# Seven products for eight in both MLP layers, over two token passes of 1024, with the second pass's token forms kept in DRAM

## The chip, the core and the metric

One NeuronCore of a Trainium2 chip runs the whole program. Its engines have instruction queues of their own, each worked off in order: TensorE (PE for the matmuls, PEld for its weight loads), VectorE (DVE), ScalarE (ACT), GpSimd (POOL) and SyncE (SP, which here issues every DMA). The metric is the device time of one execution in microseconds.

## The reference

A block with two residual branches on 2048 tokens of 576 features, float32: a spectral filter, then a two-layer MLP with a ReLU between (4608 hidden columns).

```python
def _A_ref(x, w_r, w_i):
    B, S, D = x.shape                       # 1, 2048, 576
    X = jnp.fft.rfft2(x, axes=(-2, -1)) * (w_r + 1j * w_i)
    return jnp.fft.irfft2(X, (S, D), axes=(-2, -1))

def _B_ref(x, w1, w2):                      # w1 576 x 4608, w2 4608 x 576
    h = jnp.maximum(jnp.einsum("bsd,df->bsf", x, w1), 0)
    return jnp.einsum("bsf,fd->bsd", h, w2)

h = x + _A_ref(_layernorm(x), w_r, w_i)
h2 = h + _B_ref(_layernorm(h), w1, w2)
```

## The kernel before

The transforms are matmuls with constant tables and take the first 115 us. From there a loop over 16 tiles of 128 tokens (`for t in range(NT + 6)`) ends the inverse transform (`inv_d`, `inv_a`), adds the residual into the tile `A` (`xs`), takes the layer norm (`stat2`, `norm2`) and transposes the result into `xc` (`project`).

A float32 product is made of three matmuls in float32r: an operand v is split into a high part h (a copy to float32r, on ACT) and a low part v - h (a subtraction, on DVE); a product is hh + hl + lh. `split` (L305 to L307; the copy itself is L151, in `act`) does that for weights and hidden blocks.

The MLP goes over 18 groups of 256 hidden columns (`g`) and four chunks of 512 tokens (`c`): 72 steps. `mm1` makes a step's hidden block: per 128 hidden columns 14 matmuls of 512 columns (L148, operands `xc` and the split weights). For the first eight steps `mm2` multiplies with w2 directly. From step 8 on (`WINO = 8`) `slot` does the second layer with seven products of half blocks in place of eight (Winograd's form of Strassen's algorithm): sums of the halves of the hidden block (S1 to S4) and of w2 (T1 to T4), each split; `prod` (L562) makes a product in 6 matmuls of 288 columns, and `add` (L569) adds it from PSUM into one or two quarters of `xs`. Such a slot alternates four quarters of the next step's `mm1` (7 matmuls each) with the seven products. The hidden sums are made on POOL (L547, L551 to L553), the weight sums also (L519). The order on every engine is the order in which the code is written (`manual_schedule`).

Tiles that matter: `A` the residual and result, `X` the split weight forms, `D` the split hidden forms, `e` a rotating buffer of ten, `d` four PSUM tiles of two banks.

Of the kernel before, what the change touches and what calls it, by code (L numbers as in the profile page):

```python
# [21 lines left out]
GF = 2  # L22
NG = DFF // (128 * GF)
CH = 4
NC = NT // CH
# [102 lines left out]
def kernel(ctx: ExitStack, tc: tile.TileContext, x, w_r, w_i, w1, w2, cc2, c1, fb, ib, c3, out):  # L128
    nc = tc.nc
    pool = ctx.enter_context(tc.tile_pool(name="sb", bufs=1))  # L130
    psum = ctx.enter_context(tc.tile_pool(name="ps", bufs=1, space=PSUM))

    def sb(shape, tag, bufs=1, dt=F32):
        n[0] += 1
        return pool.tile(shape, dt, tag=tag, name=f"{tag}_{n[0]}", bufs=bufs)

    n = [0]

    def ps():
# [13 lines left out]
    xs = sb([128, NT, D], "X")  # L153
# [70 lines left out]
    zx = sb([128, 5 * 2048], "A")  # L224
# [69 lines left out]
    raw, wts = {}, {}  # L294

    def load_weights(g):
        v1, v2 = ebuf([128, 5, 256]), ebuf([128, 2, D])
        f = slice(256 * g, 256 * g + 256)
        nc.sync.dma_start(v1[:, 0:4], w1[0:512, f].rearrange("(a p) f -> p a f", p=128))
        for h in range(2):  # L300
            nc.sync.dma_start(v1[64 * h:64 * h + 64, 4], w1[512:576, f])
        nc.sync.dma_start(v2, w2[f, :].rearrange("(a p) d -> p a d", p=128))
        raw[g] = (v1, v2)

    def split(h, l, v):  # L305
        act(h, v)
        nc.vector.tensor_sub(l, v, h)  # L307

    pieces = []

    def work(k):
        for _ in range(k):
            split(*pieces.pop(0))

    def split_weights(g, part):
        if g == 1 and part == 0:
            h, l = tail[0][:, 4608:5888], tail[0][:, 5888:7168]
        else:
            h, l = (ebuf([128, (1280, 1152)[part]], F32R) for _ in range(2))
        h, l = (v.rearrange("p (a n) -> p a n", a=(5, 2)[part]) for v in (h, l))  # L320
        wts[g, part] = h, l
# [304 lines left out]
    def slot(i):  # L626
# [12 lines left out]
        if w1:  # L639
            work(1)  # L640
# [130 lines left out]
```

## Time and profile before

| | |
|---|---|
| device time, median of 3 runs | 1054.95 us (1054.93 to 1055.49) |
| span of the profiled execution | 1053.3 us, of a time that is not listed apart; the median is 1.65 us above it |
| granted TensorE clock, mean | 0.994 |
| busy: PE, PEld, DVE, ACT, POOL | 1036.2, 928.0, 750.3, 389.9, 328.0 us |
| slots of the second layer in seven products | from 290 to 1047 us, 11.91 us each |
| DMA | 48.05 MB, mean 46 GB/s |

Busy times count an engine's instructions only. Matmuls overlap each other, so the duration of one (294 ns for 288 columns) is longer than the distance to the next. A group's row has line, engine, operation, written and read tiles, sizes, count, busy time and the mean of one, and then the idle time ahead of it with what ended it. A timeline row has start, duration, and the same. For back-to-back instructions the distance of two starts is the price.

### The profile page before, as it was taken

The page shows a single profiled execution, that of the slowest core. Times are in us where ns is not written, and L with a number is a line of the kernel's source. Part 1 is how long each engine was busy: PE and PEld are TensorE (multiplying, and loading weights), DVE is VectorE, ACT ScalarE, POOL GpSimd, SP SyncE. Part 2 cuts the span into 40 slices and gives each one's busy share as a digit, 9 for nine tenths or more (in the row PEclk, how much of TensorE's full clock was granted, in tenths as well). Part 3 has the DMA queues.
Part 4 walks back from the last instruction along what each step waited for, and adds up shares of the span by engine and source line. Part 5 has one row for each costly group of instructions (what it writes and reads, how often), then busy time and mean ns, then how long its engine had stood idle before and what let it go on. Part 6 is the DMA issues. An engine that isn't in the chain of part 4 may idle for free.

```text
span 1053.3 us, 17197 instructions
## 1 busy us (share of the span) xinstructions
PE 1036.2 (98%) x6560; PEld 928.0 (88%) x6560; DVE 750.3 (71%) x1409; ACT 389.9 (37%) x846; POOL 328.0 (31%) x439
## 2 busy tenths in 40 slices
PE   8999999999999999999999999999999999999997
PEld 8888778799999999999999999999999999999996
DVE  7587696543477777778777777778777777777775
ACT  4533243431133333334333333434333333434332
POOL 4300164311133424333333423333333323243322
PEclk9999999999999999999999999999999999999999
DMA  8931700011000011000000001000000001100024
GB/s 239 248 92 49 180 2 26 23 48 48 1 26 23 26 36 36 26 23 26 24 26 23 26 24 48 26 23 26 24 26 23 26 24 40 34 23 2 1 63 117
DMA packets 31105, 48.05 MB, mean 46 GB/s; under 512 B 2992, under 2 KB 22704, under 8 KB 31024
## 3 DMA queue, kind: packets, MB, share of 16 engines
q1 hardware_dynamic: 31024, 46.96, 16.5%
q8 instruction: 52, 0.85, 0.3%
q14 instruction: 29, 0.24, 0.1%
HBM read 42.23 MB, written 4.72 MB: 45 GB/s over the span
## 4 chain that ended last, share of the span: by engine, by line
PE 95%; DVE 3%; ACT 1%; issue 0%; POOL 0%; DVEq 0%; POOLq 0%; ACTq 0%
PE d L148 60%; PE d L562 33%; PE d L276 1%; PE d L446 1%; DVE A L569 0%; DVE A L428 0%; DVE e L307 0%; DVE e L416 0%; DVE e L415 0%; ACT e L222 0%; DVE e L419 0%; DVE e L360 0%; DVE e L359 0%; PE d L447 0%; DVE e L354 0%
## 5 line engine op out<-in xcount | busy, mean ns | idle before, releaser
L569 DVE TENSOR_TENSOR A<-A,d 128x576 f32<-128x576 f32 (+1 forms) x449 | 334.5, 746 | 52.6 <-PE d L562 52.5
L562 PE MATMUL d<-X,D 128*128 128x288 f32 x2304 | 345.8, 294 | 1.8 <-DVE A L569 1.7
L562 PEld LDWEIGHTS d<-X,D 128*128 128x128 f32 x2304 | 328.8, 188 | 17.3 <-issue 1.7
L148 PE MATMUL d<-B,e 128*128 128x512 f32 x952 | 238.3, 391 | 0.4 <-DVE A L428 0.4
L148 PEld LDWEIGHTS d<-B,e 128*128 128x128 f32 x952 | 172.0, 188 | 28.8 <-ACT e L151 0.8
L537 DVE SCALAR_TENSOR_TENSOR D<-d,D 128x256 fp32r<-128x256 f32 x190 | 80.7, 425 | 120.6 <-ACT D L536 120.6
L536 ACT ACTIVATE D<-d 128x256 fp32r<-128x256 f32 x190 | 72.6, 382 | 237.6 <-PE d L148 237.6
L551 POOL TENSOR_TENSOR e<-e 128x256 f32<-128x256 f32 x63 | 46.6, 739 | 349.8 <-ACT e L550 349.8
L148 PE MATMUL d<-C,e 128*128 128x512 f32 x476 | 119.1, 390 | 0.0
L148 PE MATMUL d<-X,e 128*128 128x512 f32 x476 | 118.7, 390 | 0.0
L151 ACT ACTIVATE X<-e 128x288 fp32r<-128x288 f32 (+2 forms) x177 | 70.2, 434 | 103.5 <-PE d L562 103.5
L307 DVE TENSOR_TENSOR D<-e,D 128x256 fp32r<-128x256 f32 (+1 forms) x128 | 92.6, 724 | 20.1 <-ACT D L151 20.1
L547 POOL TENSOR_TENSOR e<-e 128x256 f32<-128x256 f32 x64 | 47.5, 743 | 173.8 <-ACT e L546 170.5
L148 PEld LDWEIGHTS d<-X,e 128*128 128x128 f32 x476 | 86.0, 188 | 13.8
L148 PEld LDWEIGHTS d<-C,e 128*128 128x128 f32 x476 | 85.8, 188 | 13.7
L151 ACT ACTIVATE D<-e 128x256 fp32r<-128x256 f32 (+1 forms) x130 | 67.4, 519 | 75.3 <-POOL e L552 70.4
L307 DVE TENSOR_TENSOR X<-e,X 128x288 fp32r<-128x288 f32 (+2 forms) x176 | 82.8, 493 | 0.9 <-ACT X L151 0.9
L562 PEld LDWEIGHTS d<-X 128*128 128x128 f32 x384 | 58.0, 188 | 4.9
L562 PE MATMUL d<-X 128*128 128x288 f32 x384 | 61.3, 295 | 0.0
L148 PE MATMUL d<-e,D 128*128 128x288 f32 x384 | 55.3, 303 | 0.3 <-DVE D L480 0.3
L148 PEld LDWEIGHTS d<-e,D 128*128 128x128 f32 x384 | 53.7, 194 | 1.4 <-DVE D L480 0.6
L552 POOL TENSOR_TENSOR e<-e,e 128x256 f32<-128x256 f32 x63 | 49.7, 788 | 4.9
(85 smaller groups left out, 994.4 us busy)
## 6 DMA issues: line engine op xcount, KB each, us to landing
e<-in_B_w_dram SPq DMA_DIRECT2D x18, 576.0 KB, 3.8
e<-in_B_w_dram SPq DMA_DIRECT2D x18, 512.0 KB, 3.7
A<-in_A_x_dram SPq DMA_DIRECT2D x16, 288.0 KB, 8.2
out_dram<-A SPq DMA_DIRECT2D x30, 144.0 KB, 2.5
X<-in_A_x_dram SPq DMA_DIRECT2D x12, 288.0 KB, 7.4
e<-in_B_w_dram SPq DMA_DIRECT2D x36, 64.0 KB, 3.5
B<-in_A_w_r_dram SPq DMA_DIRECT2D x15, 144.5 KB, 7.3
B<-in_A_w_i_dram SPq DMA_DIRECT2D x15, 144.5 KB, 7.2
```

Source lines behind the costliest of these rows:

```text
L148: nc.tensor.matmul(o, l, r, start=start, stop=stop)
L151: nc.scalar.activation(o, i, AF.Copy, **kw)
L276: nc.tensor.transpose(wm[:, :128], ident, ident)
L307: nc.vector.tensor_sub(l, v, h)
L446: nc.tensor.transpose(pz[:, 128 * b:128 * b + 128], y[:, 128 * b:128 * b + 128], ident)
L536: nc.scalar.activation(h, p, AF.Relu)
L537: nc.vector.scalar_tensor_tensor(l, p, 0.0, h, op0=ALU.max, op1=ALU.subtract)
L547: nc.gpsimd.tensor_sub(fs["S3"], fs["p0"][:, 0], fs["p0"][:, 1])
L551: nc.gpsimd.tensor_add(fs["S1"], fs["p0"][:, 1], fs["p1"][:, 1])
L552: nc.gpsimd.tensor_sub(fs["S2"], fs["S1"], fs["p0"][:, 0])
L562: nc.tensor.matmul(P[:, tt], l[:, q], r, start=first and n_ == 0, stop=n_ == 2, skip_group_check=not first)
L569: nc.vector.tensor_add(xt, xt, P)
```

## The change

Both layers now use seven half-block products for eight. The tokens are taken in two passes of 1024, the hidden columns in steps of 512: 18 steps (`NS`), nine per pass, of 14 slots each. A slot is one of the first layer's seven products (`mm1`, for one of two halves u of 256 hidden columns), what combines its result (`evac`), the split of the hidden form that is needed two slots later (`form`), one product of the second layer for the step before (`prod`), and at fixed slots hidden sums and splits of weights (`tasks_old`, `tasks_new`).

- First layer: the 512 leading features and the tokens are halved; `norm2` makes four sums of the normed tokens on POOL, `project` transposes eight blocks twice per pair of tiles and splits them into seven forms `T`; the remaining 64 features stay apart in `R`. `sums1` (POOL) and `split1` make the weight forms `WF`. A product is 6 matmuls of 512 columns, plus 2 for the rest in four of the seven. Results come out of two PSUM banks, `X` and `Y`: ACT copies three partial sums (s1, u2, u3), DVE adds `Y` to them (L556), ACT applies the relu in place (L557), or reads `X` with it (L552).
- Second layer: hidden sums move from POOL to DVE (`hsum`, L520) and the products are over 512 hidden columns: 12 matmuls of 288 columns (L569) accumulate both halves `j`; the adds into `xs` are L574. Weight sums of 576 elements (`sums2`, L501) stay on POOL.
- The second pass's seven forms are written to DRAM (`Td`, 28 stores of 256 KB) while step 0 runs, and read back in step 8 (7 loads of 1 MB).
- The first layer starts at iteration 16 of the loop over tiles (iteration 10 before), since a pass needs the forms of eight tiles. PSUM: three rotating tiles `d`, and the banks `X` and `Y`, in place of four.

```diff
-GF = 2
-NG = DFF // (128 * GF)
-CH = 4
-NC = NT // CH
+NS = 18
...
+        nc.gpsimd.tensor_sub(S[:, 0], b12, b11)
+        nc.gpsimd.tensor_sub(S[:, 2], b22, b12)
+        nc.gpsimd.tensor_sub(S[:, 1], b22, S[:, 0])
+        nc.gpsimd.tensor_sub(S[:, 3], b21, S[:, 1])
+        Zs[t0 // 2] = z, S
...
+        for a, b, dst in dsts:
+            act(dst[:, :, 0], pv[:, a:b])
+            nc.vector.tensor_sub(dst[:, :, 1], pv[:, a:b], dst[:, :, 0])
...
+        if P:
+            for a, b, dst in dsts:
+                for f in range(a, b):
+                    nc.sync.dma_start(Td[f0 + f, :, :, i % 4], dst[:, f - a].rearrange("p h k n -> p (h k) n").bitcast(F32))
...
+    ORDER = (("A11", 0), ("A12", 1), ("S2", 4), ("S1", 3), ("S3", 5), ("A22", 6), ("S4", 2))
+    BANK = (0, 1, 0, 1, 0, 0, 1)
...
+    PRODS = [(n_[:2], "ab".index(n_[2])) for n_ in "P1a P2a P1b P2b P6a P5a P6b P3a P7a P5b P7b P3b P4a P4b".split()]
...
+    def form(s, k):
+        p, x = PRODS[k]
+        q = SIDE[p][0]
+        f = HF[(14 * s + k) % 4]
+        split(f[:, 0], f[:, 1], raw(s, INPLACE.get(q, q))[:, :, 256 * x:256 * x + 256])
+
+    def mm1(s, u, m):
+        a, b = ORDER[m]
+        o = M["XY"][BANK[m]]
+        ops = []
+        for k in range(2):
+            w = [WF[:, i, BLOCK[a] + k] for i in range(2)]
+            t = [T[:, b, i, k] for i in range(2)]
+            ops += [(w[0], t[0]), (w[0], t[1]), (w[1], t[0])]
...
+        for n_, (l, r) in enumerate(ops):
+            nc.tensor.matmul(o, l, r, start=first and n_ == 0, stop=n_ == len(ops) - 1, skip_group_check=not first)
+
+    def evac(s, u, m):
...
+        if m in (0, 2, 4):
+            act((s1, u2, u3)[m // 2], X)
+        if m == 5:
+            nc.scalar.activation(raw(s, q0, 1), X, AF.Relu)
+        if m in (1, 4, 6):
+            a, q, j = {1: (s1, q0, 0), 4: (u3, q1, 1), 6: (u2, q1, 0)}[m]
+            h = raw(s, q, j)
+            nc.vector.tensor_add(h, a, Y)
+            nc.scalar.activation(h, h, AF.Relu)
+
+    def prod(s, k):
...
+        for tt in range(2):
+            ops = [(l, r, j) for j in range(2) for l, r in ((0, 0), (0, 1), (1, 0))]
+            for n_, (l, r, j) in enumerate(ops):
+                nc.tensor.matmul(o[:, tt], f[:, l, j, 128 * tt:128 * tt + 128], w[:, r, j], start=first and n_ == 0,
+                                 stop=n_ == 5, skip_group_check=not first)
+        t0 = 8 * (s // 9) + c + 4 * x
+        tiles, d = slice(t0, t0 + 3, 2), slice(288 * hd, 288 * hd + 288)
+        xt = xs[:, tiles, d]
+        nc.vector.tensor_add(xt, xt, o)
...
+    def tasks_old(s, k):
+        if k == 0:
+            hsum(s, "S1", 0)
+            hsum(s, "S2", 1)
+        if k == 1:
+            hsum(s, "S2", 0)
+        if k in (2, 3):
+            split2(s, ("T2", "T1")[k - 2])
+            hsum(s, "S4", k - 2)
+        if k == 5:
+            split2(s, "B22")
+            split2(s, "T3")
+        if k == 8:
+            split2(s, "T4")
+
+    def tasks_new(s, k):
+        u, m = divmod(k, 7)
+        v = 2 * s + u
+        if v and k == 7:
+            split1(v, 1)
+        if v and k in (1, 7):
+            split1(v, 3)
+        if m == 0 and v + 2 < 2 * NS:
+            load1(v + 2)
+        if v + 1 < 2 * NS:
+            if m in (1, 2):
+                sums1(v + 1, m - 1)
+            if k in (4, 6, 10, 12, 13):
+                split1(v + 1, {4: 0, 6: 2, 10: 0, 12: 2, 13: 1}[k])
...
+        if k == 9:
+            hsum(s, "S3")
+        if k == 11:
+            split2(s, "B11")
+            sums2("T1", "T3", "T2")
+        if k == 12:
+            hsum(s, "S1", 1)
+        if k == 13:
+            split2(s, "B21")
+            sums2("T4")
+        if s == 8 and u == 1:
+            b = ORDER[m][1]
+            nc.sync.dma_start(T[:, b].rearrange("p h k n -> p (h k n)").bitcast(F32), Td[b].rearrange("p a i n -> p (a i n)"))
+
+    def slot(S, k):
+        if S < NS:
+            mm1(S, *divmod(k, 7))
+            evac(S, *divmod(k, 7))
+            if k >= 12:
+                form(S, k - 12)
+        if S:
+            if k < 12:
+                form(S - 1, k + 2)
+            prod(S - 1, k)
+            tasks_old(S - 1, k)
+        if S < NS:
+            tasks_new(S, k)
```

`split1` takes 640, 384, 512 and 640 elements for its four parts, `split2` 576, `form` 512.

What that makes of DVE's queue in the middle of the run. Before, a slot's rows: splits of hidden blocks from PSUM (L537), product adds (L569), and splits of hidden sums and weights from SBUF (L307):

```order
L537 SCALAR_TENSOR_TENSOR D_2581<-d_2580,D_2581 128x256
L569 TENSOR_TENSOR A_1268<-A_1268,d_2688 128x2x288
L537 SCALAR_TENSOR_TENSOR D_2582<-d_2580,D_2582 128x256
L569 TENSOR_TENSOR A_1268<-A_1268,d_2688 128x2x288
L307 TENSOR_TENSOR D_2583<-e_2585,D_2583 128x512
L569 TENSOR_TENSOR A_1268<-A_1268,d_2689 128x2x288
L537 SCALAR_TENSOR_TENSOR D_2581<-d_2579,D_2581 128x256
L569 TENSOR_TENSOR A_1268<-A_1268,d_2688 128x2x288
L307 TENSOR_TENSOR D_2582<-e_2585,D_2582 128x256
L569 TENSOR_TENSOR A_1268<-A_1268,d_2689 128x2x288
L307 TENSOR_TENSOR X_1872<-e_5078,X_1872 128x288 x2
L569 TENSOR_TENSOR A_1268<-A_1268,d_2688 128x2x288
```

After, the slots 11 and 12 of a step and the add that opens slot 13: the first layer's add (L556), the hidden form's split into `G` (L467), the product add (L574), the split of B11, then the next slot's form, add and tasks:

```order
L556 TENSOR_TENSOR h_4515<-u_298_1844,Y 128x512
L467 TENSOR_TENSOR G_2215<-h_4119,G_2215 128x512
L574 TENSOR_TENSOR A_1284<-A_1284,d_2218 128x2x288
L467 TENSOR_TENSOR e_2213<-e_1958,e_2213 128x576
L467 TENSOR_TENSOR HF_1851<-h_4234,HF_1851 128x512
L574 TENSOR_TENSOR A_1284<-A_1284,d_2216 128x2x288
L467 TENSOR_TENSOR WF_1288<-e_1507,WF_1288 128x512
L520 TENSOR_TENSOR h_4318<-h_4318,h_4515 128x512
L556 TENSOR_TENSOR h_4515<-u_297_1843,Y 128x512
```

Between a first-layer add and the product add behind it there is now a split that reads an ACT result. ACT's queue at the same place, before (a hidden block's relus L536, its whole relu for POOL L546 and L550, splits L151):

```order
L536 ACTIVATE D_2581<-d_2580 128x256
L550 ACTIVATE e_2584<-d_2580 128x512
L536 ACTIVATE D_2582<-d_2580 128x256
L151 ACTIVATE D_2583<-e_2585 128x512
L536 ACTIVATE D_2581<-d_2579 128x256
L546 ACTIVATE e_2584<-d_2579 128x512
L151 ACTIVATE D_2582<-e_2585 128x256
```

and after (from the partial sum u3 of slot 11 to the copy for slot 13's form):

```order
L161 ACTIVATE u_298_1844<-X 128x512
L557 ACTIVATE h_4515<-h_4515 128x512
L161 ACTIVATE G_2215<-h_4119 128x512
L161 ACTIVATE e_2213<-e_1958 128x576
L552 ACTIVATE h_4433<-X 128x512
L161 ACTIVATE HF_1851<-h_4234 128x512
L161 ACTIVATE WF_1288<-e_1507 128x512
L557 ACTIVATE h_4515<-h_4515 128x512
L161 ACTIVATE e_2117<-h_4433 128x512
```

The relu in place (L557) stands ahead of the copy of the form (L161 into `G`, `HF`, `e_2117`) of the same slot. POOL's queue in one step, before (hidden sums of a chunk, and weight sums L519):

```order
L547 TENSOR_TENSOR e_2585<-e_2584 128x256
L551 TENSOR_TENSOR e_2585<-e_2584 128x256
L552 TENSOR_TENSOR e_2585<-e_2585,e_2584 128x256
L553 TENSOR_TENSOR e_2585<-e_2584,e_2585 128x256
L519 TENSOR_TENSOR e_3229<-e_2993 128x288 x2
```

and after (weight sums of the first layer for one half, then of the second layer):

```order
L480 TENSOR_TENSOR e_1507<-e_1506 128x256
L481 TENSOR_TENSOR e_1507<-e_1507,e_1506 128x256
L483 TENSOR_TENSOR e_1507<-e_1506 128x256
L484 TENSOR_TENSOR e_1507<-e_1506,e_1507 128x256
L485 TENSOR_TENSOR e_1507<-e_1506 128x128
L501 TENSOR_TENSOR e_1958<-e_1958 128x576
L501 TENSOR_TENSOR e_1958<-e_1961,e_1958 128x576
L501 TENSOR_TENSOR T_300_1852<-e_1961,e_1958 128x576
L501 TENSOR_TENSOR e_1961<-e_1961,T_300_1852 128x576
```

The hidden sums are gone from POOL's queue, and weight sums of 576 elements stand in a row behind those of the first layer.

More of the change, by code (lines that the diff above doesn't have):

```diff
@@ L293 @@
     nc.sync.dma_start(c3t, c3)
[L294 to L321, printed above, removed]
-        for k in range((5, 2)[part]) if g >= 2 else [slice(None)]:
-            pieces.append((h[:, k], l[:, k], raw[g][part][:, k]))
-        if g <= 2:
-            work(len(pieces))
-    tail = []
-    U = sb([128, 160 * 64], "X")
+    U = sb([128, 160 * 64], "X", pool="x")
     Xs, Ys = {}, {}
@@ L692 @@
         if t % 2 == 1 and 5 <= t <= NT + 3:
[L693 removed]
+            gen = norm2(t - 5)
             next(gen)
```

473 lines of the change are left out of this document (182 added, 291 removed).

## The prediction, made before the changed kernel ran

> **What bounds the kernel now.** I read the page's busy shares and its chain of waits first.
>
> ```profile
> span 1053.3 us, 17197 instructions
> PE 1036.2 (98%) x6560; PEld 928.0 (88%) x6560; DVE 750.3 (71%) x1409; ACT 389.9 (37%) x846; POOL 328.0 (31%) x439
> ...
> PE 95%; DVE 3%; ACT 1%; issue 0%; POOL 0%; DVEq 0%; POOLq 0%; ACTq 0%
> ```
>
> TensorE (PE) is busy 98% of the span and is 95% of the chain that ended last, so PE's work is what the change can remove; the other engines matter only if one of them takes PE's place. Then the windows over four consecutive slots of the second half (start and end, then PE, PEld, DVE, ACT and POOL busy time):
>
> ```profile
> 610.34:622.25 11.91, 11.91 (x71) 10.81 (x71) 9.21 (x18) 4.93 (x12) 2.96 (x4) 1.00 0.00 1
> 622.25:634.16 11.91, 11.91 (x71) 10.81 (x71) 9.39 (x17) 4.59 (x11) 3.17 (x4) 1.00 0.18 55
> 634.16:646.07 11.91, 11.91 (x71) 10.81 (x71) 8.91 (x17) 4.51 (x11) 5.02 (x6) 1.00 0.01 2
> 646.07:657.98 11.91, 11.91 (x72) 10.80 (x71) 8.57 (x16) 4.21 (x10) 5.07 (x6) 1.00 0.18 51
> sum 47.64, PE 47.64 PEld 43.23 DVE 36.08 ACT 18.24 POOL 16.22; mean PE 11.91 PEld 10.81 DVE 9.02 ACT 4.56 POOL 4.06
> ```
>
> Four slots are 512 hidden columns for 1024 tokens, as much as one step of the changed kernel: 47.64 us, PE without a hole, DVE busy for 36.08 of them, POOL 16.22. Prices on PE, from the timeline inside a slot:
>
> ```profile
> 603.03 1.75 PE L562 MATMUL d<-X,D 128*128 128x288 f32 x12
> 604.61 1.75 PE L148 MATMUL d<-X,e 128*128 128x512 f32 x7
> 606.20 0.96 PE L562 MATMUL d<-X 128*128 128x288 f32 x6
> ```
>
> 12 products of 288 columns take 604.61 - 603.03 = 1.58 us, 0.1317 each; 7 of 512 columns take 1.59, 0.227 each. Check: 4 x (28 x 0.227 + 42 x 0.1317) = 47.5, the measured 47.64.
>
> **What the change does to PE.** The first layer goes from 14 matmuls of 512 columns per 128 hidden columns and 512 tokens (56 per 256 x 1024) to 7 x 6 + 4 x 2 = 50: 1800 in all for 2016. The second layer was already seven products for eight in all but the first eight slots: 3024 of 288 columns for 3072. A step (14 slots) costs 100 x 0.227 + 168 x 0.1317 = 44.83 us on PE, 2.8 less than four slots now. If PE stays the bound, that is the gain, 6%.
>
> **What it does to DVE, ACT and POOL.** This is where I expect the sum to be decided. Every product now reads its own split of a hidden block, the first layer needs its outputs combined, and the weights of both layers are combined and split. Durations, start to start, from timeline rows:
>
> ```profile
> 126.39 1.48 DVE L307 TENSOR_TENSOR e<-e,e 128x1280 fp32r<-128x1280 f32 x1
> 127.79 0.45 DVE L415 TENSOR_TENSOR e<-e,d 128x288 f32<-128x288 f32 x1
> ...
> 612.77 0.63 ACT L151 ACTIVATE D<-e 128x512 fp32r<-128x512 f32 x1 [1.39 <-POOL e L552]
> 613.44 0.69 DVE L307 TENSOR_TENSOR D<-e,D 128x512 fp32r<-128x512 f32 x1
> 614.04 0.75 DVE L569 TENSOR_TENSOR A<-A,d 128x576 f32<-128x576 f32 x1
> ...
> 617.70 0.74 DVE L569 TENSOR_TENSOR A<-A,d 128x576 f32<-128x576 f32 x1
> 618.36 0.82 DVE L307 TENSOR_TENSOR X<-e,X 128x288 fp32r<-128x288 f32 x2
> ...
> 621.96 0.42 DVE L537 SCALAR_TENSOR_TENSOR D<-d,D 128x256 fp32r<-128x256 f32 x1 [0.36 <-ACT D L536]
> 622.42 0.60 ACT L550 ACTIVATE e<-d 128x512 f32<-128x512 f32 x1 [0.49 <-DVE D L537]
> 622.92 0.38 ACT L536 ACTIVATE D<-d 128x256 fp32r<-128x256 f32 x1
> ```
>
> A subtraction of two SBUF operands takes 0.60 us at 512 elements (613.44 to 614.04) and 1.40 at 1280 (126.39 to 127.79), so 1.04 ns an element: 0.67 at 576, 0.73 at 640, 0.47 at 384, 1.13 at 1024. An add with one PSUM operand takes 0.66 at 576 (617.70 to 618.36), so 0.59 at 512. DVE per step: 14 product adds (L574) 9.24; 14 splits of hidden forms (L467) 8.40; 6 adds in `evac` (L556) 3.54; `hsum` (L520) 6 x 0.60 + 1.13 = 4.73; the first layer's weight splits 2 x (0.73 + 0.47 + 0.60 + 0.73) = 5.06; the second layer's 7 x 0.67 = 4.69. Sum 35.7. Slot by slot that is 2.0 to 3.2, always under PE's 2.94 (6 matmuls and a product) or 3.39 (8): taken as busy time alone DVE fits.
>
> But its queue is in order, and in the six slots with an `evac` add, what stands behind that add is the split of a hidden form; its first half is on ACT, and on ACT the relu of that same add stands ahead of it. So DVE stands still from the add's end through relu and copy. Price: the add's tail (0.74 whole against 0.66) 0.08; DVE to ACT 0.04 (621.96 + 0.42 to 622.42); the relu 0.54 (0.63 at 612.77, less the 0.10 by which ACT's next starts early, 622.42 to 622.92 for a 0.60); the copy 0.63; ACT to DVE 0.04 (612.77 + 0.63 to 613.44). 1.33, six times: 8.0. DVE's chain is 43.7 per step, against PE's 44.83. Queued behind the stopped split are the slot's product add and the weight splits; PE needs the split two slots (6.3 us) later, and at its own pace the split ends some 3 us into that time, so about 3 us of slack even out single slots and no more. ACT fits: 28 instructions of 512 elements at 0.54 and 15 first halves of weight splits at 0.7 or less are 26 us.
>
> Then POOL. Per step it makes 10 combinations of first-layer weights (8 of 256 elements, 2 of 128) and 4 of 576 for the second, at these prices:
>
> ```profile
> 616.75 0.74 POOL L547 TENSOR_TENSOR e<-e 128x256 f32<-128x256 f32 x1 [3.19 <-ACT e L546]
> 617.01 0.76 DVE L307 TENSOR_TENSOR D<-e,D 128x256 fp32r<-128x256 f32 x1 [0.31 <-ACT D L151]
> 619.78 0.42 DVE L307 TENSOR_TENSOR X<-e,X 128x256 fp32r<-128x256 f32 x1
> ...
> L307 DVE TENSOR_TENSOR D<-e,D 128x256 fp32r<-128x256 f32 x64 | 48.7, 761 | 19.5 <-ACT D L151 19.5
> L307 DVE TENSOR_TENSOR e<-e,e 128x256 fp32r<-128x256 f32 x80 | 34.0, 429 | 0.0
> L307 DVE TENSOR_TENSOR D<-e,D 128x256 fp32r<-128x256 f32 (+1 forms) x128 | 92.6, 724 | 20.1 <-ACT D L151 20.1
> L307 DVE TENSOR_TENSOR X<-e,X 128x288 fp32r<-128x288 f32 (+2 forms) x176 | 82.8, 493 | 0.9 <-ACT X L151 0.9
> ...
> 138.45 0.46 DVE L416 TENSOR_TENSOR e<-e,d 128x290 f32<-128x290 f32 x1
> 139.05 0.90 POOL L418 TENSOR_TENSOR e<-e 128x287 f32<-128x287 f32 x1 [2.08 <-DVE e L416]
> ...
> L547 POOL TENSOR_TENSOR e<-e 128x256 f32<-128x256 f32 x64 | 47.5, 743 | 173.8 <-ACT e L546 170.5 <-DVE A L569 3.2
> L454 POOL TENSOR_TENSOR B<-e,B 128x512 fp32r<-128x512 f32 x8 | 10.2, 1273 | 9.4 <-ACT e L151 9.4
> ```
>
> From 743 ns at 256 and 1273 at 512: 1.41 at 576 and 0.48 at 128, so 2 x (4 x 0.74 + 0.48) + 4 x 1.41 = 12.5 us per step. And the rows show that a DVE subtraction of two SBUF operands doesn't run while POOL works on SBUF: the one at 617.01 took 0.76 and ended 0.28 after POOL's (616.75 + 0.74), its like at 619.78 took 0.42; over 64 of them the mean is 761 ns for 429. DVE's adds from PSUM keep their 0.75 beside POOL. In the kernel before such subtractions are 92.6 + 82.8 = 175 us, 23% of 64 slots at 11.91; after, 22.9 of 44.8, 51%.
>
> Two bounds for what DVE loses per step. By share: those 64 lost 64 x 0.33 = 21 us, 1.33 per four slots or 8% of POOL's 16.22; with 51 for 23% that is 18% of 12.5, 2.3 us. By place: POOL's bursts are released by a DVE split, right ahead of more DVE work on SBUF. The worst, counted from the end of the split of B11 (POOL answers DVE 0.14 later: 138.45 + 0.46 to 139.05): the next form split holds the port to 0.69, T1's sum runs 0.69 to 2.0 under a product add that doesn't need it; the weight split that asked at 1.26 ends at 2.54 and not at 1.95; T3's sum then runs to 3.85 and the `hsum` behind it ends at 4.40, not 3.15; T2's sum falls into an `evac` gap and is free. 1.8 us; the other four bursts in the same way 1.0, 0.85, 0.55, 0.15: 4.35. I take the second, since order and releasers are known, and keep the first for the range. DVE's chain: 43.7 + 4.35 = 48.05 us, over PE's 44.83 and over the 47.64 of now.
>
> [...]
>
> **Ahead of and behind the steps.**
>
> ```profile
> 137.31 0.74 DVE L428 TENSOR_TENSOR A<-A,d 128x576 f32<-128x576 f32 x1
> 140.29 0.70 DVE L428 TENSOR_TENSOR A<-A,d 128x576 f32<-128x576 f32 x1
> 155.63 0.70 DVE L428 TENSOR_TENSOR A<-A,d 128x576 f32<-128x576 f32 x1
> 193.75 0.76 DVE L428 TENSOR_TENSOR A<-A,d 128x576 f32<-128x576 f32 x1
> ...
> 1047.57 0.82 DVE L569 TENSOR_TENSOR A<-A,d 128x288 f32<-128x288 f32 x2 [1.22 <-PE d L562]
> ```
>
> The transforms up to 137 us stay, less two weight splits on DVE (1.40, and 1.27 at 1152 elements) that move later: iteration 6's add at 140.29 comes at 137.6. From there an iteration takes 3.66 now (137.31 to 155.63, five of them, DVE without a hole); the token forms add per pair of tiles 768 + 1024 elements from PSUM and a small rest on DVE, some 1.2 per iteration less the 0.33 it did before, and 2.5 us of weight splits fall in: 9 x 4.5 + 2.5 to iteration 15, at 181, where 193.75 stands now. POOL's four token sums per pair (2.96) take the place of two L454 of 1.27. What the earlier end costs: the first layer no longer runs beside these iterations, and step 0's 100 matmuls follow in 7 more, with no products beside them.
>
> ```profile
> 137.62 0.60 PE L446 MATMUL d<-ident,e 128*128 128x128 f32 x4
> 138.05 0.27 PE L447 MATMUL d<-ident,e 128*128 128x128 f32 x1
> ...
> 50.00:60.00 10.00, 10.00 (x132) 7.80 (x130) 7.09 (x14) 2.90 (x4) 0.00 (x0) 1.00 1.06 258
> ```
>
> On PE such an iteration is 14 x 0.227 + 8 transposes at 0.11 (137.62 to 138.05, four), 4.1 us; where two products of the first layer follow each other on one PSUM bank, ACT's copy (0.60) stands between, and the rotating PSUM tiles are three for four: 5. The second pass's forms go to DRAM in 28 stores of 256 KB on SP's queue, 7.3 MB; at the 258 GB/s of the window from 50 to 60 us 28 us, at half of it (rows of 512 bytes; no row shows such) 57, in some 40 us of iterations; seven buffers that also hold step 0's hidden blocks then make ACT wait. I take 5 us, bounds 0 and 17. Step 1 starts at 181 + 2 + 7 x 5 + 5 = 223, DVE's part of it 4 us later: 227. The reload in step 8 is 7 loads of 1 MB on SP, one per slot from slot 7 on, behind PE's last read of the old form; at 4.1 us each the first has landed after 6 us and is read after 22 (seven slots), the last after 31 and is read after 42. Hidden; without that cover some 5 us once. Weight loads queued behind it on SP are issued half a step, 22 us, ahead of their use. The last step has no first layer; PE's 22.1 and DVE's 22.9 interlock to 24.4, and the last store as now takes 1053.3 - 1048.4 = 4.9. The last full step splits half a step's weights less: -2. Together 227 + 24.4 + 4.9 - 2 = 254.
>
> **Sum.** 254 + 17 x 48.05 = 1071 us of span, against 1053.3; the median of the runs lies 1.65 above that span, so 1073. It breaks even at 47.0 us per step.
>
> **Rivals.** PE stays the bound (faster): DVE's loss to POOL stays under 1.1 us per step, since POOL's sums may slide into the six gaps and under product adds; 254 + 17 x 44.83 = 1016, 1018 as a time. For it speaks that the gap per step, 8 us, could hold two thirds of POOL's 12.5; against it that the sums are released by splits and not by the gaps. Partly so: 2.3 us lost, 46.0 per step, 1036 and 1038. [...] DRAM traffic: the stores at half rate and the reload late, 17 + 5 in place of 5, 17 us more: 1090; the weight loads' cover of half a step speaks against more. That the change doesn't do what it says can be excluded for PE: the counts follow from the code.
>
> **Chances.** Forecast 0.55; PE-bound 0.14; partly 0.15; between these, within 0.2% (2 us, what a measurement of this kernel can tell from no change) 0.06; the two dearer cases 0.10. Faster 0.29, same 0.06, slower 0.65. The range leaves out PE-bound and the tail above: 1028 to 1102; the forecast's own is 1057 to 1090 (47.1 to 49 per step).
>
> **What would show it.** Windows of one step in mid-run: 48 us, PE under 95% busy, idle time of L569's or L543's matmuls ended by DVE L467 or L574; DVE waiting some 1.2 us for ACT at L467, six times a step; L467 and L520 rows of 512 elements well over 0.69 beside POOL's L501. Wrong, if a step takes 45 us and PE has no hole, or if L467's mean stays near 0.69; wrong in another place, if step 1 starts much after 223 us or the end trails the last step by more than 30.

## The result, and the profile after

The changed kernel takes 1084.54 us (median of four runs, 1083.62 to 1086.63) against 1054.94 for the kernel before on the same chip: 1.029 times as long, 95% interval 1.027 to 1.030. The forecast was 1073, slower. The profiled execution has a span of 1081.8 us. Its page begins (span, busy time by engine, shares of the chain that ended last):

```profile
span 1081.8 us, 16681 instructions
PE 1014.2 (94%) x6344; PEld 884.3 (82%) x6344; DVE 883.8 (82%) x1367; ACT 513.0 (47%) x904; POOL 357.5 (33%) x384
...
DVE 59%; PE 12%; ACT 12%; issue 12%; DMA 2%; POOL 2%; DVEq 0%; SPq 0%; ACTq 0%; POOLq 0%
```

PE fell from 95% of that chain to 12%; DVE took its place with 59%. PE's busy time fell by 22 us only. The counts (216 matmuls of 512 columns and 48 of 288 fewer, 48 transposes more), at the prediction's prices, make 50; but a step in mid-run, in the next rows, is busy for 46.2 us where those prices give 44.83. "issue" and ACT, 12% each, were nearly nothing before. Two steps in mid-run, from the same row of one step to that of the next (PE, PEld, DVE, ACT, POOL busy):

```profile
573.55:621.75 48.20, 46.24 (x270) 40.89 (x269) 40.80 (x58) 23.68 (x43) 16.30 (x15) 1.00 0.55 204
621.75:669.92 48.17, 46.23 (x270) 40.88 (x269) 40.77 (x58) 23.68 (x43) 16.29 (x15) 1.00 0.37 99
```

They are 48.2 us each. The two `hsum` rows that stand in slot 0 of every step, here of the steps 2 and 17:

```profile
284.45 2.41 DVE L520 TENSOR_TENSOR h<-h,h 128x512 f32<-128x512 f32 x2
...
1007.21 2.41 DVE L520 TENSOR_TENSOR h<-h,h 128x512 f32<-128x512 f32 x2
```

(1007.21 - 284.45) / 15 = 48.18 us per step; 48.05 was predicted. The sum has three parts, and each has its rows. First the gaps. What DVE waited for, all through the run (total, times, longest):

```profile
DVE G L467 <- ACT G L161: 65.1, 54, 1.3
DVE e L467 <- ACT e L161: 33.0, 27, 1.3
DVE HF L467 <- ACT HF L161: 31.7, 26, 1.3
```

107 waits, 1.21 us in the mean: six a step, the others in step 0. One of them, DVE and ACT side by side:

```profile
624.08 0.67 DVE L556 TENSOR_TENSOR h<-s,Y 128x512 f32<-128x512 f32 x1
624.79 0.63 ACT L557 ACTIVATE h<-h 128x512 f32<-128x512 f32 x1 [4.77 <-DVE h L556]
625.33 0.61 ACT L161 ACTIVATE G<-h 128x512 fp32r<-128x512 f32 x1
625.97 0.69 DVE L467 TENSOR_TENSOR G<-h,G 128x512 fp32r<-128x512 f32 x1 [1.22 <-ACT G L161]
626.58 0.75 DVE L574 TENSOR_TENSOR A<-A,d 128x576 f32<-128x576 f32 x1
```

The add (L556) is done at 624.75; ACT's relu (L557) follows, then the copy (L161 into `G`), and DVE's split starts 1.22 us after DVE fell idle. The product add of that slot (626.58) and all else stand behind it. Six such waits, with 1.28 for the one at 649.88, are 7.4 us.

Second, the loss to POOL ("port" in the recorded texts; the rows show that one engine waits for the other, and not what the two share). POOL's and DVE's rows around the split of B11, and the same DVE instruction where POOL rests:

```profile
660.23 1.81 POOL L501 TENSOR_TENSOR e<-e 128x576 f32<-128x576 f32 x1 [10.29 <-DVE e L467]
662.12 1.76 POOL L501 TENSOR_TENSOR e<-e,e 128x576 f32<-128x576 f32 x1
...
644.30 0.68 DVE L467 TENSOR_TENSOR WF<-e,WF 128x512 fp32r<-128x512 f32 x1
644.90 0.68 DVE L467 TENSOR_TENSOR e<-h,e 128x512 fp32r<-128x512 f32 x1
...
661.33 1.25 DVE L467 TENSOR_TENSOR WF<-e,WF 128x512 fp32r<-128x512 f32 x1
662.51 1.92 DVE L520 TENSOR_TENSOR h<-h,h 128x512 f32<-128x512 f32 x1
664.35 0.67 DVE L556 TENSOR_TENSOR h<-u,Y 128x512 f32<-128x512 f32 x1
```

The split of 512 elements takes 0.60 us from start to start at 644.30, and 1.18 at 661.33, where POOL's sum runs until 662.04; the `hsum` after it takes 1.84 for 0.60, until 0.47 after POOL's end (662.12 + 1.76). Measured in the same way, start to start against the like row where POOL rests, a step loses 0.58 + 1.24 there (slot 12), 1.13 at the two `hsum` of slot 0, 0.59 + 0.26 at the split of T2 and the `hsum` of slot 2, 0.55 at the two weight splits of slot 7: 4.35 us. The groups that lose most, with the mean of one in ns:

```profile
L520 DVE TENSOR_TENSOR h<-h,h 128x512 f32<-128x512 f32 x108 | 115.6, 1083 | 0.0
L467 DVE TENSOR_TENSOR WF<-e,WF 128x512 fp32r<-128x512 f32 x36 | 34.6, 960 | 1.2 <-ACT WF L161 1.2
L467 DVE TENSOR_TENSOR e<-T,e 128x576 fp32r<-128x576 f32 x18 | 23.5, 1305 | 0.0
```

Third, what is left is taken to be work: 48.18 - 7.4 - 4.35 = 36.4 us.

### The profile page after: what moved, and what is told of

It reads as the page before. It is cut to its first block, busy times and chain, and to the rows that moved or that the text cites. A ratio compares the mean times of both kernels' runs of the same rounds, so it can differ in the third digit from the quotient of the medians.

```text
span 1081.8 us, 16681 instructions
## 1 busy us (share of the span) xinstructions
PE 1014.2 (94%) x6344; PEld 884.3 (82%) x6344; DVE 883.8 (82%) x1367; ACT 513.0 (47%) x904; POOL 357.5 (33%) x384
## 4 chain that ended last, share of the span: by engine, by line
DVE 59%; PE 12%; ACT 12%; issue 12%; DMA 2%; POOL 2%; DVEq 0%; SPq 0%; ACTq 0%; POOLq 0%
DVE A L574 14%; DVE h L520 10%; DVE e L467 9%; DVE WF L467 8%; PE d L158 7%; DVE h L556 6%; DVE G L467 5%; ACT h L557 4%; ACT G L161 3%; DVE HF L467 3%; PE dd L158 2%; ACT HF L161 2%; ACT e L161 1%; PE d L569 1%; DMA e<-in_B_w_dram 1%
## 5 line engine op out<-in xcount | busy, mean ns | idle before, releaser
L569 PE MATMUL d<-e,G 128*128 128x288 f32 x1512 | 226.3, 296 | 19.3 <-DVE e L467 16.1
L569 PEld LDWEIGHTS d<-e,G 128*128 128x128 f32 x1512 | 212.5, 188 | 38.3 <-DVE e L467 21.3
L557 ACT ACTIVATE h<-h 128x512 f32<-128x512 f32 x108 | 68.3, 632 | 367.4 <-DVE h L556 367.0
L543 PE MATMUL X<-T,WF 128*128 128x512 f32 x864 | 225.9, 397 | 4.4 <-ACT u L161 3.3
L574 DVE TENSOR_TENSOR A<-A,d 128x576 f32<-128x576 f32 x252 | 188.3, 747 | 1.8 <-PE d L569 1.8
L543 PEld LDWEIGHTS X<-T,WF 128*128 128x128 f32 x864 | 155.2, 189 | 32.0 <-ACT u L161 4.0
L543 PE MATMUL Y<-T,WF 128*128 128x512 f32 x648 | 168.3, 395 | 3.8 <-DVE h L556 3.8
L467 DVE TENSOR_TENSOR G<-h,G 128x512 fp32r<-128x512 f32 x126 | 87.6, 695 | 65.3 <-ACT G L161 65.1
L520 DVE TENSOR_TENSOR h<-h,h 128x512 f32<-128x512 f32 (+1 forms) x126 | 137.5, 1102 | 0.0
L543 PEld LDWEIGHTS Y<-T,WF 128*128 128x128 f32 x648 | 115.8, 188 | 24.0 <-DVE h L556 4.5
L569 PE MATMUL d<-e,e 128*128 128x288 f32 x756 | 113.9, 297 | 13.3 <-DVE e L467 9.8
L569 PEld LDWEIGHTS d<-e,e 128*128 128x128 f32 x756 | 105.9, 188 | 24.6 <-DVE e L467 11.9
L467 DVE TENSOR_TENSOR WF<-e,WF 128x640 fp32r<-128x640 f32 (+2 forms) x144 | 121.9, 858 | 3.2 <-ACT WF L161 3.2
L569 PE MATMUL d<-e,HF 128*128 128x288 f32 x756 | 113.0, 296 | 4.8 <-DVE e L467 4.7
L569 PEld LDWEIGHTS d<-e,HF 128*128 128x128 f32 x756 | 106.7, 188 | 12.9 <-DVE e L467 7.7
L501 POOL TENSOR_TENSOR e<-e 128x576 f32<-128x576 f32 x18 | 32.3, 1796 | 192.8 <-DVE e L467 192.8
L161 ACT ACTIVATE WF<-e 128x640 fp32r<-128x640 f32 (+2 forms) x144 | 90.8, 644 | 0.0
L161 ACT ACTIVATE G<-h 128x512 fp32r<-128x512 f32 x126 | 77.9, 619 | 16.1 <-DVE h L520 14.0
L467 DVE TENSOR_TENSOR e<-e,e 128x576 fp32r<-128x576 f32 x108 | 79.7, 752 | 1.3 <-ACT e L161 1.3
L161 ACT ACTIVATE e<-e 128x576 fp32r<-128x576 f32 x108 | 70.6, 670 | 0.0
L467 DVE TENSOR_TENSOR HF<-h,HF 128x512 fp32r<-128x512 f32 x63 | 44.2, 702 | 31.9 <-ACT HF L161 31.7
## 6 DMA issues: line engine op xcount, KB each, us to landing
T<-Td SPq DMA_DIRECT2D x7, 1024.0 KB, 10.4
```

Source lines behind the costliest of these rows:

```text
L161: nc.scalar.activation(o, i, AF.Copy, **kw)
L501: nc.gpsimd.tensor_sub(d, a, b)
L520: f(raw(s, d, j), raw(s, a, j), raw(s, b, j))
L543: nc.tensor.matmul(o, l, r, start=first and n_ == 0, stop=n_ == len(ops) - 1, skip_group_check=not first)
L557: nc.scalar.activation(h, h, AF.Relu)
L569: nc.tensor.matmul(o[:, tt], f[:, l, j, 128 * tt:128 * tt + 128], w[:, r, j], start=first and n_ == 0, stop=n_ == 5, skip_group_check=not ...
```

## The experiments

Four theories were to be told apart. A is the prediction's: DVE's in-order chain is the step, and gaps and loss to POOL each add to it. B: they are slack, and PE or the weights' arrival sets the pace. C: gaps and losses to POOL overlap, so that one returns when the other goes. D: traffic with DRAM carries the loss. S is on the start of step 1 alone: that ACT and DVE wait for each other in the token forms. Times are medians of four or five runs, ratios are to the kernel before on the same chip.

**The hidden form's split ahead of the first layer's add, on both queues** (`e1_form_first`).

```diff
             mm1(S, *divmod(k, 7))
-            evac(S, *divmod(k, 7))
             if k >= 12:
                 form(S, k - 12)
-        if S:
-            if k < 12:
-                form(S - 1, k + 2)
+        if S and k < 12:
+            form(S - 1, k + 2)
+        if S < NS:
+            evac(S, *divmod(k, 7))
+        if S:
             prod(S - 1, k)
```

> The changed kernel with one edit: in every slot the split of the hidden form stands ahead of the first layer's evacuation, on ACT and on DVE, so that the copy is not behind the relu and DVE does not stand still between the add and the split. Theory A (DVE's in-order chain sets the step: 36.3 us of work, six gaps of 1.23 = 7.4, 4.5 lost to POOL = 48.18): the gaps go, the chain falls to 40.8 us, under PE's 44.83, and PE sets the pace: 17 x (48.18 - 44.83) = 57 us less than 1084.5, so 1028 (1024 to 1040), PE without a hole. Rival B (PE, the weights' arrival or DRAM traffic sets the step and the gaps are only DVE's slack): the wait turns up on other rows, 1075 to 1085. Rival C (the splits, freed from the gaps, now meet POOL's sums, which lay in the gaps): port loss up to 8, chain 44.3 and uneven, 46 per step, about 1047.

Measured 1049.25 us, ratio 0.995 (0.993 to 0.997): 35 us less than the changed kernel, a little faster than before. A's direction, C's number. The waits at the hidden forms are gone, and a step takes 45.9 us (45.84 to 46.06 in the 15 steps). Why not 44.8, two pieces of the timeline show, of DVE and of PE:

```profile
514.05 2.41 DVE L520 TENSOR_TENSOR h<-h,h 128x512 f32<-128x512 f32 x2
516.39 1.22 DVE L467 TENSOR_TENSOR G<-h,G 128x512 fp32r<-128x512 f32 x1
517.53 0.68 DVE L556 TENSOR_TENSOR h<-s,Y 128x512 f32<-128x512 f32 x1
...
518.26 1.63 PE L543 MATMUL Y<-T,WF 128*128 128x512 f32 x6 [0.34 <-DVE h L556]
```

The `hsum` pair of slot 0 meets POOL as before (2.34 us for 1.20 alone), and so does now the form's split behind it (1.14 for 0.60), which in the changed kernel started after its wait, at 625.97, when POOL's sums had ended (623.69 + 1.07). The add L556, which gives the bank Y back, stands behind that split, and PE's next product in Y waits 0.34 us. So C names a wait that is there, but a small one: 6.2 us in the 15 steps from 300 to 1020 us, 0.4 each. The rest of what a step takes above 44.83 is PE's own pace, which the next two runs give; that C's number fits is in part luck.

**POOL's weight sums cut to 16 columns after the first ones** (`e2_thin_pool`), the remainder of the sums left out; and **both edits** (`e3_both`).

```diff
-        t, S = V1[v % 2], M["SW"]
-        A11, ... = (t[:, 2 * k:2 * k + 2, 128 * f:128 * f + 128] ...
+        n = 16 if v else 128
+        t, S = V1[v % 2], M["SW"][:, :, :n]
+        A11, ... = (t[:, 2 * k:2 * k + 2, 128 * f:128 * f + n] ...
...
-            d, a, b = (V2[x] for x in o[n_])
+            d, a, b = (V2[x][:, :, :288 if s == 0 else 16] for x in o[n_])
```

> The changed kernel with POOL's weight sums cut to 16 columns per block after the first ones (the rest of these sums is left out): the order and all waits stay, POOL's time on SBUF nearly goes. Theory A: DVE's chain loses its 4.5 us of port loss, 43.7 per step, 1.1 under PE's 44.83; single slots longer than 3 us hold PE up a little, 45 to 46 per step: 1084.5 - 17 x 2.7 = 1039 (1028 to 1050). Rival B (the gaps or PE set the pace, and the blocked splits only fill waits): 1075 or more.

> Both edits, the forms ahead of the evacuations and POOL's weight sums cut to 16 columns (the rest of them left out). Theory A: DVE's chain is 36.3 us per step, far under PE's 44.83, so this is PE's own pace: 1027, within 5 us of the version with the forms ahead alone. If the port loss still costs where DVE is no longer the bound, this is more than 8 us faster than that version. Rival B: 1065 or more.

Measured 1034.93 (ratio 0.982, 0.981 to 0.984) and 1031.84 (0.978, 0.977 to 0.980). With the order and the waits of the changed kernel, but without most of POOL's work (4.91 us busy a step for 16.30), 50 us are gone. The groups of DVE that had lost most, in the first of the two (lines are one higher there):

```profile
L521 DVE TENSOR_TENSOR h<-h,h 128x512 f32<-128x512 f32 x108 | 72.3, 683 | 0.0
L467 DVE TENSOR_TENSOR WF<-e,WF 128x512 fp32r<-128x512 f32 x36 | 25.4, 705 | 1.2 <-ACT WF L161 1.2
L467 DVE TENSOR_TENSOR e<-T,e 128x576 fp32r<-128x576 f32 x18 | 13.5, 750 | 0.0
```

1083 became 683 ns, 960 became 705, and 1305 became 750, while the waits at L467 stayed, 65.1 us at `G` alone. In neither kernel does DVE wait for a result of POOL between 300 and 1000 us, so that it isn't the sums' earlier arrival that helps. So POOL's work beside them was the price of these rows, and the 43.8 us of chain that are left fit under PE. B falls. Both edits together bring 3 us more than POOL's alone, no more than the runs of one such kernel differ (1030.3 to 1036.3): with DVE no longer the bound, neither term costs more than that here. What then bounds, PE's rows of the two kernels show, without a hole:

```profile
484.48 1.53 PE L544 MATMUL Y<-T,WF 128*128 128x512 f32 x6
485.85 0.62 PE L544 MATMUL Y<-R,WF 128*128 128x512 f32 x2
486.30 1.76 PE L570 MATMUL d<-e,G 128*128 128x288 f32 x12
487.90 1.53 PE L544 MATMUL X<-T,WF 128*128 128x512 f32 x6
...
483.28 1.56 PE L544 MATMUL Y<-T,WF 128*128 128x512 f32 x6
484.68 0.62 PE L544 MATMUL Y<-R,WF 128*128 128x512 f32 x2
485.14 1.75 PE L570 MATMUL d<-e,G 128*128 128x288 f32 x12
486.73 1.56 PE L544 MATMUL X<-T,WF 128*128 128x512 f32 x6
```

In the first kernel eight matmuls of 512 columns take 1.82 us (484.48 to 486.30), in the second 1.86 (483.28 to 485.14), 0.228 and 0.233 each; twelve of 288 columns take 1.60 and 1.59. That makes 45.16 and 45.45 us per step: PE's own pace has two values here. Both stand in one trace, that of the version with the forms first, which changes from one to the other at the wait shown above. The version with the copy first (below) took 1034.6 us once and 1040.8 three times; 17 x 0.29 is 4.9 of the 6.2 between. Only one of its four runs was profiled (1040.8, with 45.45), so that these are the two paces is likely and not shown, and what chooses between them stays open.

**No traffic with DRAM for the second pass** (`e4_no_dram`): stores and reload of the token forms are left out, the second pass uses those of the first.

```diff
-        if P:
-            for a, b, dst in dsts:
-                for f in range(a, b):
-                    nc.sync.dma_start(Td[f0 + f, :, :, i % 4], ...)
...
-        if s == 8 and u == 1:
-            ...
-            nc.sync.dma_start(T[:, b]..., Td[b]...)
```

> The changed kernel without the stores of the second pass's token forms to DRAM and without their reload (the second pass then works on the first pass's forms, and those of the second are left out). Theory A: the steps stay at 48.18 us, the reload was hidden; only step 0, where ACT waited for buffers that a store still read, gets up to 8 us shorter: 1077 to 1084. Rival D (DRAM traffic carries the loss): 1067 or less, and a shorter step 8.

Measured 1085.43 (ratio 1.030, 1.028 to 1.031): no change, and the first product add comes no earlier:

```profile
237.54 0.74 DVE L570 TENSOR_TENSOR A<-A,d 128x576 f32<-128x576 f32 x1
```

28 stores of 256 KB and 7 loads of 1024 KB cost nothing: 1084.54 us with them. Theory D falls, and with it the 5 us that the prediction had set down for the stores. The half rate it allowed them was the author's estimate, which no run shows; in the changed kernel a store lands 3.1 us after its issue, in the median.

**ACT's queue alone** (`f1_copy_first`): the copy of the hidden form ahead of the relu, DVE's order as in the changed kernel. `form` is cut in two, part 0 (ACT's copy) and part 1 (DVE's subtraction).

```diff
             mm1(S, *divmod(k, 7))
+            if k >= 12:
+                form(S, k - 12, 0)
+        if S and k < 12:
+            form(S - 1, k + 2, 0)
+        if S < NS:
             evac(S, *divmod(k, 7))
             if k >= 12:
-                form(S, k - 12)
+                form(S, k - 12, 1)
         if S:
             if k < 12:
-                form(S - 1, k + 2)
+                form(S - 1, k + 2, 1)
             prod(S - 1, k)
```

> The changed kernel with one edit on ACT's queue alone: the copy (first half) of the hidden form stands ahead of the relu of the first layer's add; DVE's order is that of the changed kernel (add, split, product add). Theory A (six times a step DVE waits out relu and copy behind its add): the copy is there before the add ends, the six waits of 1.22 us at L467 are gone, DVE's chain is 48.18 - 7.4 = 40.8 us and PE sets the pace, 45.2 to 45.5 us a step as without POOL's sums; against the version with the whole form first, whose PE waited some 0.4 us a step for the add L556, DVE gives the bank back earlier: 1038 to 1046. Rival (it was DVE's order, not ACT's, that mattered): the waits at L467 stay over 0.5 us, 1060 or more.

Measured 1040.82 (ratio 0.986, 0.983 to 0.989), 44 us less than the changed kernel. Its page and its waits from 300 to 1000 us:

```profile
PE 86%; DVE 7%; POOL 2%; ACT 2%; issue 1%; DMA 1%; SPq 0%; ACTq 0%; POOLq 0%; DVEq 0%
...
DVE A L578 <- PE d L573: 56.6, 64, 1.1
```

DVE's waits for ACT at L467 are gone, and what stands in their place is DVE waiting for products of PE. POOL's sums run as before and cost nothing now: 40.8 us of chain with the loss to POOL in it lie under PE's pace. The add keeps its place, so the bank comes back in time, and PE waits for nothing; the step is 45.45 us in the profiled run. It was ACT's order that made the gaps. By the traces the 17 steps are 46.2 us shorter, and the start 3.4 us longer (the first product add comes at 240.12 for 236.74); where these 3.4 come from stays open.

**The start: ACT's copies of the token forms ahead of DVE's subtractions** (`f2_acts_first`).

```diff
         for a, b, dst in dsts:
             act(dst[:, :, 0], pv[:, a:b])
-            nc.vector.tensor_sub(dst[:, :, 1], pv[:, a:b], dst[:, :, 0])
         if part == 0:
             rp = pz[64:128, 768:].rearrange("p (c n) -> p c n", c=2)
             act(R[P][64:128, :, q], rp)
+        for a, b, dst in dsts:
+            nc.vector.tensor_sub(dst[:, :, 1], pv[:, a:b], dst[:, :, 0])
+        if part == 0:
             nc.vector.tensor_sub(R[P][0:64, :, q], rp, R[P][64:128, :, q])
```

> The changed kernel with one edit ahead of the steps: in each token form ACT's copies all stand ahead of DVE's subtractions (before, copy and subtraction of the parts alternated, and DVE waited for ACT 0.4 to 1.2 us and ACT for DVE as long). Theory S (the start is 9.7 us later than predicted because of these waits in both directions, which I had costed at nothing): step 1's first product add comes 5 to 10 us earlier than 236.7, the steps stay 48.18, 1075 to 1080. Rival (DVE's and POOL's work in these iterations, or PE's lower granted clock after its holes, sets the start): within 2 us of 1084.5.

Measured 1078.71 (ratio 1.023, 1.022 to 1.025), 5.8 us less. The first product add (line 576 here) shows where:

```profile
231.76 0.74 DVE L576 TENSOR_TENSOR A<-A,d 128x576 f32<-128x576 f32 x1
```

5.0 us earlier than the 236.74 of the changed kernel; a step is still 48.18. Of ACT's waits up to 237 us those for DVE's L443 (9.8 us at R, 9.3 at h, 2.0 at R) are gone, and part of them has moved to the relu L559 (13.9 for 7.4).

**PE's clock at the start** (`f3_warm`): 16 transposes that nothing reads, ahead of the second half of the inverse transform in iterations 12, 15 and 16.

```diff
+        if t in (12, 15, 16):
+            warm_pe(16)
         if 0 <= t - 1 < NT:
             inv_a(t - 1)
```

> The changed kernel with 16 transposes without use on PE ahead of the inverse transform's second half in iterations 12, 15 and 16, to fill holes after which the profile shows a granted clock of 0.5 to 0.74 in 164-172 and 184-192 us. If the lower clock is what delays the start: PE's clock stays near 1, step 0's first six products take 1.4 us for 3.05, the start comes 2 to 4 us earlier, 1081. If DVE and POOL set the start: within 1 us of 1084.5, or 1 to 2 us later through the added work.

The granted clock (third column from the right) around these iterations, of the changed kernel and of this one:

```profile
168.00:172.00 4.00, 4.00 (x20) 3.38 (x19) 3.29 (x7) 1.53 (x3) 2.88 (x7) 0.74 0.00 0
184.00:188.00 4.00, 2.27 (x5) 1.33 (x5) 3.48 (x8) 0.38 (x1) 2.90 (x4) 0.50 0.00 0
188.00:192.00 4.00, 4.00 (x13) 3.10 (x13) 2.24 (x6) 1.84 (x3) 1.44 (x4) 0.68 0.83 219
```

```profile
168.00:172.00 4.00, 4.00 (x26) 3.45 (x25) 3.90 (x8) 2.02 (x4) 2.96 (x7) 1.00 0.00 0
184.00:188.00 4.00, 3.50 (x21) 2.76 (x20) 3.07 (x8) 1.22 (x4) 2.16 (x3) 1.00 0.07 19
188.00:192.00 4.00, 4.00 (x23) 3.37 (x22) 2.64 (x6) 2.13 (x4) 1.45 (x4) 1.00 0.99 271
```

The clock stays at 1.00, and the first six products of step 0 take 1.60 us (186.67 to 188.27) for 2.89 (187.74 to 190.63); the first product add comes at 234.41. Measured 1083.05 (ratio 1.027, 1.026 to 1.029), 1.5 us less than the changed kernel (1.027 to 1.030): the intervals overlap, so a gain is not shown; the trace's 2.3 us at the first product add agrees in sign.

**Edits together.** `f4_cand` has both copies first and, as a third edit, POOL's first weight sums in iterations 9 and 11 in place of both in 10; `g1_copy_acts` leaves the third out; `g2_cand_warm` adds 16 transposes in iterations 15 and 16 to the three.

```diff
-        if t == 10:
+        if t == 9:
             sums1(0, 0)
+        if t == 11:
             sums1(0, 1)
```

> The changed kernel with three edits: ACT's copy of the hidden form ahead of the relu, ACT's copies of the token forms ahead of DVE's subtractions, and POOL's first weight sums split over iterations 9 and 11, in which POOL has no token sums (PE had waited 3.7 us at 161 for a POOL operation behind them). If the parts add up: the time of the version with the copy first less 5 to 10 for the token forms less 2 for POOL, 1028 to 1038, below both kernels. If the start is not set by these: that version's time, within 3 us.

> The version of three edits without the third: ACT's copy of the hidden form ahead of the relu and ACT's copies of the token forms ahead of DVE's subtractions, POOL's first weight sums both in iteration 10 as in the changed kernel. If the two edits only add up: 1040.8 - 5.8 = 1035, and the third edit is worth the other 10 us to 1025.1. If the third is worth only the 2 to 3 us of PE's hole behind POOL at 161 us: 1028, and the two edits give more together than apart (the step's pace of 45.16 in place of 45.45 would be 5 of it).

> The version of three edits with 16 transposes without use on PE in iterations 15 and 16, where its profile shows a granted clock of 0.62 to 0.70 from 177 to 187 us, after holes of 1 to 2 us. If the lowered clock lengthens the start there: 1022 to 1024 against 1025.1 (14 products of 512 columns at 0.62 lose 2 us). If DVE and POOL set that stretch: within 1 us of it.

Measured 1025.14 (ratio 0.974, 0.972 to 0.976), 1028.30 (0.976, 0.973 to 0.979) and 1023.75 (0.971, 0.969 to 0.973). The two edits add up if the copy first is taken at its quicker run, 1034.6 - 5.8 = 1028.8. In the profiled executions, 1038.9 us with the copy first and 1027.2 with both, the first product add comes 7.7 us earlier (232.40 for 240.12), which is more than the 5.0 that the second edit gave alone, and the steps are 4.3 us shorter in all, since PE runs at 45.16 in place of 45.45. The medians of the third edit and of the transposes are 3.2 and 1.4 us lower, with intervals that overlap; the first product add comes at 228.62 and 227.17, 3.8 and 1.45 us earlier. The last is the quickest of all: 31 us less than the kernel before, 61 less than the changed one. Its page:

```profile
span 1021.7 us, 16781 instructions
PE 994.7 (97%) x6376; PEld 888.3 (87%) x6376; DVE 893.6 (87%) x1367; ACT 516.6 (51%) x904; POOL 355.6 (35%) x384
...
PE 87%; DVE 7%; DMA 1%; issue 1%; POOL 1%; ACT 1%; SPq 0%; ACTq 0%; DVEq 0%; POOLq 0%
```

PE is 97% busy and 87% of the chain again, with 41 us less of busy time than in the kernel before (994.7 for 1036.2).

## Why the prediction held, and the step that failed

- PE's work per step, 44.83 us: shown only where PE sets the pace, 45.16 or 45.45. The price of 0.227 was 0.2 to 2.4% too low (1.82 / 8 and 1.86 / 8), that of 0.1317 about 1%. It cost the forecast nothing, since PE wasn't the bound; the rival "PE stays the bound" would have been 1023 to 1028 on this term, for 1018.
- DVE's work, 35.7: 36.4 remains when waits and loss to POOL are taken off. Some 0.5 of it are the tails of six adds (0.08 each), which the prediction had put into the gaps. So the step came within 0.13 us partly because these two terms miss in opposite directions.
- The `evac` gaps, 6 x 1.33 = 8.0: 7.4 in the waits. That they are a cause and not only idle time is shown by the version that moves ACT's copies alone: 44 us.
- POOL's work, 12.5 us a step: 16.3. Its rows lengthen as well where they meet DVE's: a sum of 256 elements takes 1.13 us at 645.06, beside DVE's split, and 0.74 at 648.08, beside an add from PSUM and a gap. No engine waited for POOL between 300 and 1000 us. In the kernel before, a sum of 288 elements (L519) takes 1.28 us at 649.32, where DVE's split of 512 runs from 649.24 to 649.93, and 0.81 in the median.
- The loss to POOL, 4.35 by place against 2.3 by share: 4.35. The bursts that the prediction priced at 1.8, 1.0, 0.85, 0.55 and 0.15 measure 1.82, 1.13, 0.85, 0.55 and nothing. Choosing the bound that follows order and releasers was right, and the version with thin sums shows the loss as a cause: 50 us.
- Either remedy alone is enough, which the sum implied and did not say: the chain is 3.0 us longer than PE's 45.16, and taking off 7.4 or 4.35 puts it under PE. The effects of 44 and 50 us don't add (the forms first and the thin sums together: 53), and neither is the price of its term.
- DVE's rows beside POOL's: at 661.33 and 662.51 they end 0.47 us after POOL's, where 0.60 is their time alone, 0.13 less; in the row at 617.01, on which the prediction rested, 0.28 stands for 0.42, 0.14 less. No run shows either of the two dearer cases of its chances: the loss was the 4.35 us a step of the forecast, and the traffic with DRAM cost nothing.
- The marks: the six waits of 1.2 us, the L520 and L467 rows well over 0.69 and the step of 48 us came. "PE under 95% busy" did not quite: the windows have 46.2 of 48.2 us, 96%, the page 94%.

The step that failed is the start: "9 x 4.5 + 2.5 to iteration 15, at 181" and "Step 1 starts at 181 + 2 + 7 x 5 + 5 = 223, DVE's part of it 4 us later: 227". Iteration 6's add came at 138.22 for 137.6, iteration 15's at 185.82 (the 193.75 that the prediction sets beside it is iteration 16's; 15's is at 188.67 in the kernel before, and the sum uses neither), PE's step 1 at 226.73, DVE's first product add at 236.74, 10.0 us behind PE where 4 were set down. So the sign "step 1 starts much after 223" was there in a small measure on PE and in full on DVE. The iterations were costed by busy time, with ACT's copy and DVE's subtraction of a token form following each other at no price, the very thing that the `evac` gaps had been charged for. The rows, from step 0:

```profile
193.99 0.58 ACT L161 ACTIVATE h<-d 128x512 fp32r<-128x512 f32 x1
194.60 0.69 DVE L443 TENSOR_TENSOR h<-d,h 128x512 fp32r<-128x512 f32 x1 [1.18 <-ACT h L161]
195.33 0.60 ACT L161 ACTIVATE h<-d 128x512 fp32r<-128x512 f32 x1 [0.76 <-DVE h L443]
195.96 0.69 DVE L443 TENSOR_TENSOR h<-d,h 128x512 fp32r<-128x512 f32 x1 [0.67 <-ACT h L161]
...
226.73 1.65 PE L543 MATMUL X<-T,WF 128*128 128x512 f32 x6 [1.13 <-ACT h L552]
...
231.88 0.69 DVE L467 TENSOR_TENSOR e<-h,e 128x512 fp32r<-128x512 f32 x1 [1.22 <-ACT e L161]
...
236.74 0.74 DVE L574 TENSOR_TENSOR A<-A,d 128x576 f32<-128x576 f32 x1
```

ACT's second copy starts when DVE's first subtraction has ended (194.60 + 0.69), and DVE then waits 0.67 us for it. Since the 5 us set down for the stores weren't there, the miss is 14.7 us and not 9.7: 4.8 up to iteration 15, 3.9 from there to PE's step 1, 6.0 in DVE's distance behind PE. At the first product add the order of these copies gave 5.0 us alone and 7.7 on top of the copy of the hidden form, POOL's sums 3.8, the clock 1.45 or 2.3: 10 to 13 of the 14.7. The smallest of these is not clear of chance: iteration 15's add, which lies ahead of their edits, comes between 185.65 and 187.02 us in the traces of the changed kernel and of the first five versions that share its start. The rest stays open. With the copies first DVE still waits 8.3 us for ACT at these subtractions up to 237 us; and the gap behind a first-layer add, which the sum charged for the steps alone, stands in step 0 too: 1.18, 1.22, 1.27 and 1.22 us at 194.60, 209.34, 222.97 and 231.88. No run takes these alone away.

The sum: 17 x 0.13 = 2.2 for the steps, 9.7 for the start, -1.3 for the end (1081.8 - 236.7 - 17 x 48.18 = 26.0, for 24.4 + 4.9 - 2), and 1.1 more between span and median make 11.7, which but for rounding are the 11.5 us between 1073 and 1084.5. The -1.3 is not the end itself, which takes 29.9 for 29.3: step 1 is 1.1 us shorter than the others (47.05), since no sum of POOL meets its first `hsum`, and the last full step 2.8 (45.41) for the 2 set down.

## What to carry to other kernels

A term costed once (ACT and DVE taking turns in order) has to be looked for at every place where the same pair of instructions stands, the start included. Before a new split or relu goes on an in-order queue, write down what its consumer's queue holds behind it: here two lines of order on ACT decided between 3% slower and over 1% faster, with the same work on every engine. And when a chain exceeds the next bound by a little, any one of its terms is worth only the excess: compare chains, not terms.

## What the runs showed of the hardware that was not expected

- The granted clock of PE fell to 0.50 to 0.74 in stretches of 4 us after holes of 1.8 to 3.7 us in its work (168 to 172 and 184 to 192 us of the changed kernel), and stayed at 1.00 with 16 transposes in each of three holes. The kernel before has no such hole there, and 1.00. The medians are 1.4 to 1.5 us lower without the drops, which is not clear of their scatter. The first drop came behind a hole of 3.7 us, the second behind holes of 2.1 and 1.8 us with 1.1 us of transposes between. The version with the added transposes keeps waits of up to 2.8 us on PE between 137 and 237 us, and its mean clock over the profiled execution is 1.000. What it is about a hole that lowers the clock these runs don't tell.
- PE's matmuls of 512 columns have two paces, 0.228 and 0.233 us, for the same instructions, with a granted clock of 1.00 in both; over a run that is some 5 us, so that two versions that PE bounds can't be told apart more closely by single runs.
- Stores of 256 KB that land in 3.1 us and loads of 1024 KB in 10.4 us, each in the median, left no mark on the time: without them it was 1085.43 us for 1084.54.
